# Score maximum in a spare PSUM column, sum scaling as a step, and an order of work drawn up anew: attention and a two-layer network on one core

## The chip, the cores and the metric

The kernel runs on one core of one Trainium2 chip. A core has five queues that run side by side, each in its own order: TensorE (PE in the profile, PEld for its weight loads), VectorE (DVE), ScalarE (ACT), GpSimd (POOL) and SyncE (SP), which here only issues transfers. Matmuls write their results into PSUM, all other tiles lie in SBUF. The metric is the device time of one execution in microseconds (us).

## The reference

Queries, keys and values have shape (4, 8, 768, 64): 4 batches, 8 heads, 768 positions, 64 numbers a head. Each query and key gets a bucket of 6 sign bits; a query attends only to keys of its own bucket. The attention output, reordered to 3072 rows of 512, goes through a network of 512 to 2048 to 512 with GELU between.

```python
q_bits = (np.einsum('bhsd,dk->bhsk', q, proj) > 0)      # k_bits alike
mask = q_bucket[:, :, :, None] == k_bucket[:, :, None, :]
scores = np.where(mask, scale * q @ k.T, -1000000000.0)
scores = scores - np.max(scores, axis=-1, keepdims=True)
attn = np.exp(scores)
attn = attn / (np.sum(attn, axis=-1, keepdims=True) + 1e-09)
x = (attn @ v).transpose(0, 2, 1, 3).reshape(B * S, H * D)
h = x @ w_in
g = 0.5 * h * (1.0 + erf(h / sqrt(2)))
return g @ w_out
```

## The kernel before, in words

**Score tiles.** One unit of attention (`unit`, L750) is 128 queries of one head against all 768 keys; there are 192 units. `scores` (L760) makes 2 x 2 matmuls into a score tile `s` in PSUM: two halves of 384 columns, each at the start of its own bank of 512, so that 128 columns of either bank are unused. There are two such tiles. The mask is part of the same matmuls: extra rows of the operands add 0 where the 6 bits agree and a large negative number, a multiple of `BIG / 2` = 2^33, where they don't. `top` (L767) is a DVE reduction over the tile, which writes the negated maximum `nm` into `rows`, a small SBUF tile of seven numbers a row. `guard` (L770) is a DVE instruction on two elements: it multiplies the pair (1, `nm`) by 1, or by 0 where `nm` shows that no key had the query's bucket, and so makes the scale `sc` and the bias `nb`. `exps` (L777) is the exponential on ACT, which takes both and also adds up the row's sum `ssum`; only then is the score tile free for another unit. `si` is the sum times a power of two plus the small constant, and `norm` (L785) its reciprocal `r` on DVE. The table `SI` (L30) says where `si` is computed: for batch 0 on ACT, in the same step as the exponential; for batches 1 to 3 on DVE, in the same step as the reciprocal.

**Two ways onward.** A unit of the "whole" kind (the four head pairs of the first pass and two of the second, `WHOLE`, L28) is transposed on PE against a diagonal that holds `r` (`whole_turn`, L825; matmuls of L834), copied out of PSUM (ACT or DVE), and multiplied with the values in fp32 (L882). Every other unit is split into a high and a low fp16 half (`high`, L790, on ACT, DVE or POOL; `low`, L793, on DVE), transposed by a transfer that SP issues (`turn`, L799, the DMA at L801), and multiplied with the values' halves (L891).

**Passes.** The first pass takes 256 queries of all 8 heads of batch 0, the second the other 512, three more take batches 1 to 3. Beside them the weights are loaded, decoded on DVE, scaled and split (`weight_pair`, L447; `w_in` in four jobs, then `w_out` in four, through three `wraw` buffers in that order), and the scale of the values is found (`v_scale`, L564). The network runs on groups of 256 rows and 8 blocks of the hidden layer: hidden matmuls (L1076), scaling out of PSUM on ACT (L1086), GELU (L1110, which needs another table on ACT than the exponential), a split of the result, output matmuls (L1144), and at the end of a row block `drain` (L1164) and `store`. The network of one batch fills PE while attention of later ones goes on; it needs all of `w_in` decoded for its first hidden matmul and all of `w_out` for its first output matmul.

**The order.** Nothing is scheduled by hand. Each step is given to a planner (`Plan`, L52) with a cost in us, what it needs, the buffer that it takes, and a key; a step that may run on several engines has a cost and a key offset for each. `order` (L91) plays the steps through with these costs: an engine that is free takes the ready step of lowest key. The instructions are then emitted in that order, so that each engine's queue is fixed in advance, and a queue whose next instruction isn't ready waits. The keys are a unit's running number (or a constant) plus offsets from `PAR` (L33). `HOP`, `SAME` and others are the plan's costs for handing on a result; `port` marks DVE steps that the plan keeps apart from POOL's.

Of the kernel before, what the change touches and what calls it, by code (L numbers as in the profile page):

```python
# [10 lines left out]
F32 = mybir.dt.float32  # L11
# [17 lines left out]
TABLE = 1.3  # L29
SI = ("ACT", "ACT", "DVE")  # L30
GROW = ("p","hl")

PAR = dict(Z=268.47, VS0=1.21, H0=215.64, HL=-15.55, VS=-265.71, G2=6.63, HQ=-12.55, VQ=-4.7, in0=-73.45, out0=510.52, in1=114.3, out1=-23.2, in2=-152.73, out2=90.41, in3=-266.67, out3=305.62, H1=156.76, H2=26.31, H3=-124.25, H4=-47.37, H5=96.79, H6=-21.71, H7=-18.75, MEV=-10, MGE=-10, MSP=-9, V0=28.21, QK0=31.02, QK1=11.42, QK2=-140.46, MX0=-80.33, MX1=9.9, MX2=-171.5, EX0=-27.01, EX1=10.79, EX2=61.01, NR0=17.61, NR1=-25.22, NR2=244.7, HI0=-71.29, HI1=35.16, HI2=6.43, LO0=-34.27, LO1=80.28, LO2=111.56, PV0=285.55, PV1=4.61, PV2=4.07, TR0=-68.6, TR1=51.33, TR2=-109.76, V1=-165.36, V2=-260.64, Sin0=88.02, Sin1=-15.33, Sin2=43.2, Sin3=-128.94, Sout0=71.1, Sout1=-10.94, Sout2=100.15, Sout3=-147.52, Lin=-134.59, Pin=-24.26, Qin=-42.42, Cin=-52.71, Min=-68.37, Lout=-123.13, Pout=189.72, Qout=-194.24, Cout=-82.99, Mout=284.13, G0=46.99, G1=276.82, G3=31.32, G4=-297.54, G5=-122.96, G6=-106.16, G7=-15.81, DUP0=-55.86, DUP1=-36.2, DUP2=101.92, LOW0=-29.55, LOW1=24.48, LOW2=24.75, PRJ0=106.61, PRJ1=8.12, PRJ2=140.3, MSK0=53.6, MSK1=-45.87, MSK2=-170.2, DI_ACT=152.6, DI_DVE=8.86, DI_Pool=-7.82, WS_ACT=62.38, WS_DVE=-70.95, WS_Pool=66.08, WH_ACT=24.68, WH_DVE=71.89, WH_Pool=-16.12, WL_ACT=167.53, WL_DVE=-13.6, WL_Pool=-46.06, VH_ACT=274.75, VH_DVE=33.02, VH_Pool=-33.68, MV_SP=-11.58, MV_ACT=170.85, MV_DVE=0.62, MV_Pool=-22.12, LO_ACT=16.2, LO_DVE=-202.51, LO_Pool=30.98, RND_ACT=-26.8, RND_DVE=128.78, RND_Pool=11.96, MSK_ACT=111.97, MSK_DVE=17.48, MSK_Pool=8.92, HI_ACT=-61.13, HI_DVE=-30.23, HI_Pool=15.87, DG_ACT=-0.18, DG_DVE=-102.45, DG_Pool=-90.6, EV_ACT=-12.47, EV_DVE=-6.28, EV_Pool=-230.2, GH_ACT=-45.74, GH_DVE=58.43, GH_Pool=56.03)  # L33
BIG = 2.0**34
# [3 lines left out]
class Step:  # L38
    def __init__(self, seq, engine, cost, emit, key, needs, takes, table, port):
# [5 lines left out]
        self.takes, self.table, self.port = takes, table, port  # L45
        self.needs = [n for n in needs if n is not None]
        self.slot = None
        self.frees = []
        self.start = self.end = None


class Plan:  # L52
# [14 lines left out]
    QUEUE = 2.0  # L67
    PORT = 0.1
    WINDOW = 3.413

    def __init__(self, rings):
        self.rings = {name: list(range(n)) for name, n in rings.items()}
        self.steps = []

    def add(self, engine, cost, emit, key, needs=(), takes=None, table=None, port=False):
        s = Step(len(self.steps), engine, cost, emit, key, needs, takes, table, port)
        self.steps.append(s)
        return s
# [12 lines left out]
    def order(self):  # L91
# [28 lines left out]
        port_at, port_of = 0.0, None  # L120
        warm, window, busy = False, 0, {}
        for t in set(free_at.values()):
            heapq.heappush(events, (t, -1, None))
        count = 0
        while events:
# [4 lines left out]
            for e in batch:  # L130
                if e is None:
                    continue
                for hold in e.frees:
                    hold["left"] -= 1
                    if not hold["left"]:
                        self.rings[hold["holder"].takes].append(hold["holder"].slot)
                for u in users.get(e, ()):
                    left[u] -= 1
                    for w in u.ways:
                        hop = self.SAME.get(w, 0.05) if w == e.engine else self.HOP[e.engine] + 0.12 * (w == "Pool")  # L140
                        at[u, w] = max(at.get((u, w), 0.0), now + hop)
                        heapq.heappush(events, (at[u, w], -1, None))
                    if not left[u]:
                        enlist(u)
            for engine, pool in ready.items():
# [3 lines left out]
                for s in pool:  # L149
                    if at.get((s, engine), 0.0) > now:  # L150
                        continue
                    if s.takes and not self.rings[s.takes]:
# [15 lines left out]
                if s.takes:  # L168
                    s.slot = self.rings[s.takes].pop(0)
# [24 lines left out]
                if engine == "SP":  # L194
                    free_at[engine] = now + 0.65
                    dma_at = max(dma_at, now + 1.0) + cost
# [19 lines left out]
def tile_bucket_attention_moe(  # L216
# [533 lines left out]
    def unit(t, i, q0, qs, cl, whole, made, place):  # L750

        aq, ak, bq, bk = sets[i]
        st = rows[:, t % NT]
        nm, sc, nb, ssum, si, r = (st[:, k : k + 1] for k in range(1, 7))

# [11 lines left out]
        def top():  # L767
            nc.vector.tensor_reduce(out=nm, in_=both(sp), axis=AX.XY, op=ALU.max, negate=True)  # L768

        def guard():  # L770

            nc.vector.scalar_tensor_tensor(  # L772
                out=st[:, 2:4], in0=nm.broadcast_to([P, 2]), scalar=BIG / 2, in1=st[:, :2],
                op0=ALU.is_lt, op1=ALU.mult,
            )

        def exps():  # L777
# [3 lines left out]
            )  # L781
            if si_on == "ACT":
                affine("ACT", si, ssum, unity, 1e-9 * unity)

        def norm():  # L785
            if si_on == "DVE":
                affine("DVE", si, ssum, unity, 1e-9 * unity)
            nc.vector.reciprocal(out=r, in_=si)
# [36 lines left out]
    def whole_turn(ex, nr, r, place, cl, t):  # L825
# [41 lines left out]
    def values(b, pr, ch, whole, vhl, turns, holds, key):  # L867
# [357 lines left out]
```

## Time and profile before

| What | Value |
|---|---|
| Three runs | 946.87, 948.25 and 949.5 us; median 948.25 |
| Profiled execution | span 946.1 us from the first to the last instruction; no other time is noted for it |
| PE busy | 874.5 us, 92% |
| DVE busy | 737.3 us, 78% |
| ACT busy | 595.7 us, 63% |
| POOL busy | 237.7 us, 25% |
| Last attention unit's exponential | starts at about 754 us |
| Mean granted clock of PE | 0.978 |

How to read the rows that follow in the prediction. A group's row names line, engine, operation, the tiles written and read, their shapes and the count; behind the first bar stand busy time in us and the mean of one in ns, behind the second the engine's idle time just before these instructions and what ended it. Many steps share the helper lines L382 (ACT) and L385 (DVE or POOL), so that the tile's name tells them apart. The row of a source line has the shortest, median and longest duration in ns, and the first and last start. A wait's row has who waited for whom, the total in us, how often, and the longest. A row of the timeline has start and duration in us.

### The profile page before, as it was taken

Reading aid. Unit: us, or ns where it says so; the run is one execution under the profiler, and the core shown is the slowest. Engines: PE = TensorE matmul, PEld = TensorE weight load, DVE = VectorE, ACT = ScalarE, POOL = GpSimd, SP = SyncE. Lnnn points to the kernel's source line nnn. Section 1 sums busy time; section 2 is a strip of 40 time slices with the busy share of each in tenths; the row PEclk is TensorE's granted clock in tenths of the full one; section 3 lists DMA queues with packets and bytes.
Section 4 is the critical chain, followed back from the end, with each engine's and each line's share of the span. In section 5 each row is a group of like instructions: output and inputs, shape, how many; then the busy total and the mean of one; then the engine's idle time right before and its main releaser. Section 6 shows DMA issues by size and latency. Waiting matters only on the chain. (4 is left out here: it accounts for less than half of the span.)

```text
span 946.1 us, 17526 instructions
## 1 busy us (share of the span) xinstructions
PE 874.5 (92%) x6656; PEld 636.7 (67%) x6656; DVE 737.3 (78%) x1455; ACT 595.7 (63%) x949; POOL 237.7 (25%) x230
## 2 busy tenths in 40 slices
PE   3764899969999999999999999999999999999998
PEld 2653787856767767687767676775777766676763
DVE  7989999998999999989899998899998822212122
ACT  5565677878777786778878766767776623222221
POOL 2321222344332433313324223222344200000000
PEclk9796999989999999999999999999999999999999
DMA  8575751588999799788988987869775830000000
GB/s 251 161 229 149 208 165 52 128 183 157 152 180 177 159 181 210 154 163 160 176 167 163 209 161 150 163 118 178 154 151 121 138 58 23 1 24 23 1 24 22
DMA packets 314628, 128.81 MB, mean 136 GB/s; under 512 B 254128, under 2 KB 298288, under 8 KB 314544
## 3 DMA queue, kind: packets, MB, share of 16 engines
q1 hardware_dynamic: 314368, 127.70, 64.0%
q8 instruction: 52, 0.85, 0.4%
q14 instruction: 32, 0.26, 0.1%
q10 hardware_dynamic: 176, 0.00, 0.0%
HBM read 45.49 MB, written 6.29 MB: 55 GB/s over the span
## 5 line engine op out<-in xcount | busy, mean ns | idle before, releaser
L1076 PE MATMUL hp<-x,Win 128*128 128x256 f16 x2304 | 268.6, 274 | 1.3 <-DVE x L918 0.7
L1144 PE MATMUL hp<-Wout,g 128*128 128x512 f16 x1152 | 262.3, 380 | 0.4 <-DVE g L1124 0.4
L1076 PEld LDWEIGHTS <-Win 128*128 128x128 f16 x2304 | 220.5, 98 | 43.8 <-issue 15.0
L1144 PEld LDWEIGHTS <-g 128*128 128x128 f16 x1152 | 108.4, 98 | 128.4 <-issue 9.3
L768 DVE TENSOR_REDUCE rows<-s 128x1 f32<-128x768 f32 x192 | 179.7, 949 | 7.9 <-PE s L765 6.8
L778 ACT ACTIVATE p<-s,rows 128x768 f32<-128x768 f32 x140 | 138.3, 988 | 43.3 <-DVE rows L772 28.5
L764 PE MATMUL s<-Ak,Aq 128*128 128x384 f32 x352 | 137.2, 390 | 17.5 <-ACT p L778 11.1
L1086 ACT ACTIVATE h<-hp,ffs 128x512 f32<-128x512 f32 x96 | 65.6, 683 | 118.8 <-PE hp L1076 118.3
L765 PE MATMUL s<-Bk,Bq 128*128 128x384 f32 x352 | 120.3, 342 | 0.0
L385 DVE TENSOR_SCALAR g<-h,ffs 128x512 f16<-128x512 f32 x33 | 18.5, 561 | 122.2 <-ACT h L1110 86.8
L764 PEld LDWEIGHTS s<-Ak,Aq 128*128 128x128 f32 x352 | 67.2, 191 | 42.7 <-ACT p L778 17.8
L891 PE MATMUL hp<-pt,vhl 128*64 128x256 f16 x1440 | 86.4, 274 | 4.5 <-DMA pt<-hl 2.3
L891 PEld LDWEIGHTS <-vhl 128*64 128x64 f16 x1440 | 76.5, 110 | 16.1 <-issue 12.5
L794 DVE SCALAR_TENSOR_TENSOR hl<-p,rows,hl 128x768 f16<-128x768 f32 x71 | 73.6, 1038 | 2.8 <-POOL hl L385 1.7
L1124 DVE SCALAR_TENSOR_TENSOR g<-h,ffs,g 128x512 f16<-128x512 f32 x96 | 72.3, 768 | 3.9 <-POOL g L385 1.1
L765 PEld LDWEIGHTS s<-Bk,Bq 128*128 128x128 f32 x352 | 67.7, 192 | 0.8
L385 POOL TENSOR_SCALAR hl<-p,rows 128x768 f16<-128x768 f32 x38 | 42.5, 1119 | 100.1 <-DMA pt<-hl 42.4
L834 PEld LDWEIGHTS hp<-dr,p 128*128 128x128 f32 x384 | 53.1, 218 | 20.2 <-ACT dr L382 9.9
L834 PE MATMUL hp<-dr,p 128*128 128x128 f32 x384 | 56.7, 308 | 10.5 <-POOL dr L385 6.3
L778 ACT ACTIVATE wraw<-s,rows 128x768 f32<-128x768 f32 x52 | 51.4, 988 | 18.6 <-DVE rows L772 9.2
L729 ACT ACTIVATE sign<-hp,off 44x256 f32<-44x256 f32 (+1 forms) x74 | 41.9, 574 | 29.6 <-PE hp L726 28.7
L772 DVE SCALAR_TENSOR_TENSOR rows<-rows 128x2 f32<-128x2 f32 x192 | 52.1, 277 | 1.0
(164 smaller groups left out, 1151.8 us busy)
## 6 DMA issues: line engine op xcount, KB each, us to landing
raw<-qk SPq DMA_DIRECT2D x29, 384.0 KB, 3.4
vraw<-v SPq DMA_DIRECT2D x26, 384.0 KB, 4.0
wraw<-w_in SPq DMA_DIRECT2D x16, 512.0 KB, 4.9
wraw<-w_out SPq DMA_DIRECT2D x16, 512.0 KB, 4.9
out<-o SPq DMA_DIRECT2D x12, 512.0 KB, 2.8
Bk<-Aq SPq DMA_DIRECT2D x18, 192.0 KB, 3.6
Ak<-Aq SPq DMA_DIRECT2D x18, 192.0 KB, 3.2
rawe<-qk SPq DMA_DIRECT2D x8, 384.0 KB, 4.7
```

Source lines behind the costliest of these rows:

```text
L385: on.tensor_scalar(out=out, in0=in_, scalar1=scale, scalar2=bias, op0=ALU.mult, op1=ALU.add)
L764: nc.tensor.matmul(to, aq[:, qs], ak[:, n], start=True, stop=False)
L765: nc.tensor.matmul(to, bq[:, qs.start - q0 : qs.stop - q0], bk[:, n], start=False, stop=True)
L768: nc.vector.tensor_reduce(out=nm, in_=both(sp), axis=AX.XY, op=ALU.max, negate=True)
L778: nc.scalar.activation(out=buf(ex).rearrange("p (b k) -> p b k", b=2), in_=both(sp), func=AF.Exp, scale=sc, bias=nb, accum_out=ssum,)
L794: nc.vector.scalar_tensor_tensor(out=buf(hi)[:, 1], in0=buf(ex), scalar=r, in1=buf(hi)[:, 0], op0=ALU.mult, op1=ALU.subtract,)
L834: nc.tensor.matmul(buf(step[0])[:, (k - k0) * P : (k - k0 + 1) * P], buf(ex)[:, words(k)], buf(dg), start=True, stop=True,)
L891: nc.tensor.matmul(pv[j * D : (j + 1) * D], buf(vh)[:, tv, kt, j * D : (j + 1) * D], buf(holds[j][0])[:, tp * KT + kt, :nt], start=kt == 0 ...
L1076: nc.tensor.matmul(buf(pair[0])[:, j * ch[1] : (j + 1) * ch[1]], win_hl[:, f0 // WB1, tw, pr, f0 % WB1 : f0 % WB1 + P], x[:, tx, pr, : ch[1]],
L1086: nc.scalar.activation(out=bufs["h"][0][:, 2 * fp : 2 * fp + 2, :nt], in_=buf(pair[0])[:, : 2 * nt].rearrange("p (j k) -> p j k", j=2), fu ...
L1124: nc.vector.scalar_tensor_tensor(out=gt[:, 1, s2, :nt], in0=h[:, s2, :nt], scalar=sg, in1=gt[:, 0, s2, :nt], op0=ALU.mult, op1=ALU.subtract,)
L1144: nc.tensor.matmul(buf(banks[u]).rearrange("p (c f) -> p c f", c=NWB), gt[:, tg, f, u * P : (u + 1) * P], wout_hl[:, :, tw, ft], start=ft ...
```

## The change

It has these parts:

- `top` writes the negated maximum into column 385 of the score tile itself, in PSUM; column 384 holds a 1.0, written into both tiles by DVE at the start. `guard` reads the pair from there as its second tensor; its first tensor is a constant SBUF pair `limit` of `BIG / 2`, and its scalar is the maximum's column. `rows` shrinks from seven numbers to five.
- Scaling the sum is a step of its own (`total`), between the exponential and the reciprocal, which the planner gives to ACT, DVE or POOL; `SI` goes.
- The plan's costs change: scores 0.72 to 0.7, fp32 transposes 0.214 to 0.223 a block, fp16 value matmuls 0.72 to 0.655, 0.09 for a switch of PE between those and all others, the transposing transfer 2.16 to 2.0 with 1.6 us of SP in place of 0.65 (all other transfers 0.55), another hop by engine (`HOPX`), and a buffer that comes free only one hop after its last reader.
- All offsets in `PAR` are others. With them every engine's order differs.

Which computations are done, and in what precision, stays the same.

```diff
-SI = ("ACT", "ACT", "DVE")
-PAR = dict(Z=268.47, VS0=1.21, H0=215.64, HL=-15.55, VS=-265.71, G2=6.63, ...
-    in0=-73.45, out0=510.52, in1=114.3, out1=-23.2, in2=-152.73, out2=90.41, in3=-266.67, out3=305.62, ...
-    QK0=31.02, ... MX0=-80.33, MX1=9.9, MX2=-171.5, ... Sin0=88.02, ...
+PAR = dict(SI0=289.56, SI1=-565.22, SI2=403.39, SI_ACT=-600, SI_DVE=-170.18, SI_Pool=36.23,
+    Z=135.98, VS0=600, H0=204.16, HL=-220.19, VS=-592.65, G2=360.64, ...
+    in0=370.71, out0=600, in1=535.3, out1=27.1, in2=-394.38, out2=235.52, in3=-469.93, out3=579.09, ...
+    QK0=548.05, ... MX0=-466.08, MX1=114.98, MX2=-557.52, ... Sin0=530.47, ...
+HOPX = {"PE": 0.0, "DVE": -0.0, "ACT": -0.05, "Pool": 0.23, "SP": 0.15}
...
-                        self.rings[hold["holder"].takes].append(hold["holder"].slot)
+                        at_ = now + self.HOP[e.engine]
+                        self.rings[hold["holder"].takes].append((hold["holder"].slot, at_))
...
-                        hop = self.SAME.get(w, 0.05) if w == e.engine else self.HOP[e.engine] + 0.12 * (w == "Pool")
+                        hop = self.SAME.get(w, 0.05) if w == e.engine else self.HOP[e.engine] + HOPX.get(e.engine, 0.0) + 0.12 * (w == "Pool")
...
                 if engine == "PE":
+                    cost += self.SWITCH * (s.half != half)
+                    half = s.half
...
-                    free_at[engine] = now + 0.65
+                    free_at[engine] = now + s.issue
...
-    rows = const.tile([P, NT, 7], F32, tag="rows", name="rows")
+    rows = const.tile([P, NT, 5], F32, tag="rows", name="rows")
...
-    nc.gpsimd.memset(rows[:, :, 0], 1.0)
+    limit = const.tile([P, 2], F32, tag="limit", name="limit")
+    nc.gpsimd.memset(limit, BIG / 2)
+    SPARE = S // 2
+    for t in bufs["s"]:
+        nc.vector.memset(t[:, SPARE : SPARE + 1], 1.0)
...
-        nm, sc, nb, ssum, si, r = (st[:, k : k + 1] for k in range(1, 7))
+        sc, nb, ssum, si, r = (st[:, k : k + 1] for k in range(5))
...
         def top():
-            nc.vector.tensor_reduce(out=nm, in_=both(sp), axis=AX.XY, op=ALU.max, negate=True)
+            nc.vector.tensor_reduce(out=buf(sp)[:, SPARE + 1 : SPARE + 2], in_=both(sp), axis=AX.XY, op=ALU.max, negate=True)
         def guard():
             nc.vector.scalar_tensor_tensor(
-                out=st[:, 2:4], in0=nm.broadcast_to([P, 2]), scalar=BIG / 2, in1=st[:, :2],
-                op0=ALU.is_lt, op1=ALU.mult,
+                out=st[:, :2], in0=limit, scalar=buf(sp)[:, SPARE + 1 : SPARE + 2],
+                in1=buf(sp)[:, SPARE : SPARE + 2], op0=ALU.is_gt, op1=ALU.mult,
             )
...
-            if si_on == "ACT":
-                affine("ACT", si, ssum, unity, 1e-9 * unity)
+        def total():
+            affine(su.engine, si, ssum, unity, 1e-9 * unity)
         def norm():
-            if si_on == "DVE":
-                affine("DVE", si, ssum, unity, 1e-9 * unity)
             nc.vector.reciprocal(out=r, in_=si)
...
-        sp = add("PE", 0.72, scores, t - PAR[f"QK{cl}"], made, takes="s")
+        sp = add("PE", 0.7, scores, t - PAR[f"QK{cl}"], made, takes="s")
...
-        ex = add("ACT", 0.98 + 0.23 * (si_on == "ACT"), exps, t - PAR[f"EX{cl}"], [sh], takes="p", table="exp")
+        ex = add("ACT", 0.98, exps, t - PAR[f"EX{cl}"], [sh], takes="p", table="exp")
-        nr = add("DVE", 0.07 + 0.2 * (si_on == "DVE"), norm, t - PAR[f"NR{cl}"], [ex])
+        su = add({e: (c, PAR[f"SI_{e}"]) for e, c in (("ACT", 0.23), ("DVE", 0.07), ("Pool", 0.16))}, 0, total, t - PAR[f"SI{cl}"], [ex])
+        nr = add("DVE", 0.07, norm, t - PAR[f"NR{cl}"], [su])
...
-        tr = add("SP", 2.16, turn, t + PAR[f"TR{cl}"], [lo, *hold[:1]], takes=None if hold else "pt")
+        tr = add("SP", 2.0, turn, t + PAR[f"TR{cl}"], [lo, *hold[:1]], takes=None if hold else "pt", issue=1.6)
...
-                add("PE", 0.214 * (k1 - k0), lambda ...: product(k0, k1, step), t + PAR[f"LO{cl}"], [dg], takes="hp")
+                add("PE", 0.223 * (k1 - k0), lambda ...: product(k0, k1, step), t + PAR[f"LO{cl}"], [dg], takes="hp")
...
-                    "PE", (0.9 if whole else 0.72) * nt / TC, ..., takes=None if n else "hp",
+                    "PE", (0.9 if whole else 0.655) * nt / TC, ..., takes=None if n else "hp", half=True,
```

More of the change, by code (lines that the diff above doesn't have):

```diff
@@ new lines @@
+PAR = dict(SI0=289.56, SI1=-565.22, SI2=403.39, SI_ACT=-600, SI_DVE=-170.18, SI_Pool=36.23, Z=135.98, VS0=600, H0=204.16, HL=-220.19, VS=-592.65, G2=360.64, HQ=36.42, VQ=-419.48, in0=370.71, out0=600, in1=535.3, out1=27.1, in2=-394.38, out2=235.52, in3=-469.93, out3=579.09, H1=527.91, H2=-321.61, H3=79.43, H4=449.56, H5=505.15, H6=277.36, H7=420.57, MEV=433.8, MGE=387.64, MSP=347.76, V0=582.83, QK0=548.05, QK1=-95.08, QK2=-470.18, MX0=-466.08, MX1=114.98, MX2=-557.52, EX0=-202.79, EX1=194.78, EX2=-11.92, NR0=223.22, NR1=-104.15, NR2=269, HI0=396.2, HI1=-476.56, HI2=409.28, LO0=507.4, LO1=291.25, LO2=395.17, PV0=548.55, PV1=499.49, PV2=45.4, TR0=-278.97, TR1=320.43, TR2=452.27, V1=-222.57, V2=-600, Sin0=530.47, Sin1=-600, Sin2=-206.79, Sin3=-204.7, Sout0=-293.17, Sout1=24.18, Sout2=426.41, Sout3=40.21, Lin=-306.18, Pin=233.47, Qin=-256.16, Cin=27.08, Min=-219.73, Lout=592.14, Pout=489.27, Qout=-465.81, Cout=27.6, Mout=146.07, G0=-62.95, G1=-73.22, G3=486.95, G4=-472.28, G5=54.41, G6=565.59, G7=-205.73, DUP0=45.38, DUP1=155.05, DUP2=-162.47, LOW0=432.39, LOW1=-135.42, LOW2=209.52, PRJ0=513.66, PRJ1=22.94, PRJ2=142.76, MSK0=185.96, MSK1=-399.14, MSK2=590.75, DI_ACT=305.84, DI_DVE=-107.45, DI_Pool=-220.1, WS_ACT=-600, WS_DVE=147.75, WS_Pool=446.41, WH_ACT=-418.38, WH_DVE=342.62, WH_Pool=-124.86, WL_ACT=29.63, WL_DVE=161.85, WL_Pool=-128.43, VH_ACT=-462.83, VH_DVE=81.56, VH_Pool=-9.85, MV_SP=518.36, MV_ACT=504.85, MV_DVE=-13.84, MV_Pool=511.1, LO_ACT=-600, LO_DVE=-2.05, LO_Pool=-600, RND_ACT=240.8, RND_DVE=35.59, RND_Pool=-145.02, MSK_ACT=453.53, MSK_DVE=279.08, MSK_Pool=586.93, HI_ACT=121.96, HI_DVE=351.82, HI_Pool=-341.52, DG_ACT=558.51, DG_DVE=46.22, DG_Pool=-132.65, EV_ACT=-260.46, EV_DVE=-26.08, EV_Pool=-59.11, GH_ACT=-21.44, GH_DVE=-600, GH_Pool=388.78)
@@ L38, with __init__ @@
 class Step:
-    def __init__(self, seq, engine, cost, emit, key, needs, takes, table, port):
+    def __init__(self, seq, engine, cost, emit, key, needs, takes, table, port, half=False, issue=0.55):
         many = isinstance(engine, dict)
@@ L45, in __init__ @@
         self.takes, self.table, self.port = takes, table, port
+        self.half, self.issue = half, issue
         self.needs = [n for n in needs if n is not None]
@@ L68, with add @@
     PORT = 0.1
+    SWITCH = 0.09
     WINDOW = 3.413
     def __init__(self, rings):
-        self.rings = {name: list(range(n)) for name, n in rings.items()}
+        self.rings = {name: [(k, 0.0) for k in range(n)] for name, n in rings.items()}
         self.steps = []
-    def add(self, engine, cost, emit, key, needs=(), takes=None, table=None, port=False):
-        s = Step(len(self.steps), engine, cost, emit, key, needs, takes, table, port)
+    def add(self, engine, cost, emit, key, needs=(), takes=None, table=None, port=False, half=False, issue=0.55):
+        s = Step(len(self.steps), engine, cost, emit, key, needs, takes, table, port, half, issue)
         self.steps.append(s)
@@ L121, in order @@
         warm, window, busy = False, 0, {}
+        half = False
         for t in set(free_at.values()):
@@ L135, in order @@
                     if not hold["left"]:
-                        self.rings[hold["holder"].takes].append(hold["holder"].slot)
+                        at_ = now + self.HOP[e.engine]
+                        self.rings[hold["holder"].takes].append((hold["holder"].slot, at_))
+                        heapq.heappush(events, (at_, -1, None))
                 for u in users.get(e, ()):
@@ L151, in order @@
                         continue
-                    if s.takes and not self.rings[s.takes]:
+                    if s.takes and not (self.rings[s.takes] and self.rings[s.takes][0][1] <= now):
                         continue
@@ L168, in order @@
                 if s.takes:
-                    s.slot = self.rings[s.takes].pop(0)
+                    s.slot = self.rings[s.takes].pop(0)[0]
                     head[s.takes] += 1
@@ L806, in unit @@
         unity = 1.0 if whole else 2.0**-15
-        si_on = SI[cl]
-        sp = add("PE", 0.72, scores, t - PAR[f"QK{cl}"], made, takes="s")
+        sp = add("PE", 0.7, scores, t - PAR[f"QK{cl}"], made, takes="s")
         mx = add("DVE", 0.87, top, t - PAR[f"MX{cl}"], [sp])
         sh = add("DVE", 0.07, guard, t - PAR[f"EX{cl}"], [mx])
-        ex = add("ACT", 0.98 + 0.23 * (si_on == "ACT"), exps, t - PAR[f"EX{cl}"], [sh], takes="p", table="exp")
+        ex = add("ACT", 0.98, exps, t - PAR[f"EX{cl}"], [sh], takes="p", table="exp")
         free(sp, [ex])
-        nr = add("DVE", 0.07 + 0.2 * (si_on == "DVE"), norm, t - PAR[f"NR{cl}"], [ex])
+        su = add({e: (c, PAR[f"SI_{e}"]) for e, c in (("ACT", 0.23), ("DVE", 0.07), ("Pool", 0.16))}, 0, total, t - PAR[f"SI{cl}"], [ex])
+        nr = add("DVE", 0.07, norm, t - PAR[f"NR{cl}"], [su])
         if whole:
@@ L850, in whole_turn @@
             step.append(
-                add("PE", 0.214 * (k1 - k0), lambda k0=k0, k1=k1, step=step: product(k0, k1, step), t + PAR[f"LO{cl}"], [dg], takes="hp")
+                add("PE", 0.223 * (k1 - k0), lambda k0=k0, k1=k1, step=step: product(k0, k1, step), t + PAR[f"LO{cl}"], [dg], takes="hp")
             )
@@ L902, in values @@
                 add(
-                    "PE", (0.9 if whole else 0.72) * nt / TC, lambda kts=kts: product(kts), key, [vh, vl, xt[b, ch], *turns, *parts],
-                    takes=None if n else "hp",
+                    "PE", (0.9 if whole else 0.655) * nt / TC, lambda kts=kts: product(kts), key, [vh, vl, xt[b, ch], *turns, *parts],
+                    takes=None if n else "hp", half=True,
                 )
```

1 line of the change is left out of this document (removed).

## The prediction

> **What bounds the kernel now.** I read the totals and the stages first. Outside the profiled span of 946.1 us lie 2.15 us, if the median of the three runs (948.25) stands for an execution like the profiled one; the sum below is made against 946.1 and those 2.15 are added at its end.
>
> ```profile
> span 946.1 us, 17526 instructions
> PE 874.5 (92%) x6656; PEld 636.7 (67%) x6656; DVE 737.3 (78%) x1455; ACT 595.7 (63%) x949; POOL 237.7 (25%) x230
> ```
>
> The stages, in columns of time, PE, PEld, DVE, ACT and POOL busy time with instruction counts, granted PE clock, DMA share and GB/s:
>
> ```profile
> 0.00:10.00 10.00, 0.95 (x3) 0.39 (x4) 4.66 (x11) 4.32 (x5) 3.75 (x14) 1.00 0.77 200
> 0.00:130.00 130.00, 87.10 (x587) 70.32 (x588) 113.37 (x236) 76.14 (x145) 33.24 (x48) 0.88 0.67 192
> 130.00:250.00 120.00, 107.52 (x845) 82.48 (x844) 113.54 (x226) 93.49 (x170) 41.53 (x42) 0.96 0.65 141
> 250.00:750.00 500.00, 488.85 (x3888) 357.70 (x3886) 459.48 (x913) 372.16 (x575) 160.50 (x139) 1.00 0.85 164
> 750.00:946.00 196.00, 191.05 (x1343) 126.18 (x1340) 50.92 (x83) 53.90 (x62) 2.44 (x2) 1.00 0.10 24
> ```
>
> TensorE sets the end. Its work is the same matmuls before and after the change, so only its idle time and its slow clock can be won. Idle, as length minus busy: 42.9 us in the first 130, 12.5 from 130 to 250, 11.2 from 250 to 750, 5.0 after that. The rest of the kernel matters as far as it feeds PE. In the first two stages DVE is the feeder and nearly full: behind its first 10 us (4.66 busy) it works 108.7 of 120 us, then 113.5 of 120. From 250 on the hidden and output matmuls fill PE whatever attention does. The waits of PE, first those to 100 us, then 100 to 250, then 250 to 760 (total, times, longest):
>
> ```profile
> PE s L764 <- ACT p L778: 7.6, 2, 6.8
> ...
> PE s L764 <- ACT wraw L778: 6.8, 2, 4.9
> ...
> PE s L764 <- ACT p L778: 3.1, 6, 1.0
> PE s L764 <- ACT wraw L778: 2.4, 3, 1.1
> ```
>
> The score matmul (L764) waits for the exponential that frees one of two score tiles, and that exponential waits for maximum and guard. How such a gap is made:
>
> ```profile
> 194.40 1.91 ACT L1110 ACTIVATE h<-h 128x2048 f32<-128x2048 f32 x1
> ...
> 195.08 2.59 POOL L405 TENSOR_TENSOR Bk<-raw,Aq 64x768 fp32r<-64x768 f32 x1
> ...
> 195.94 1.76 DVE L772 SCALAR_TENSOR_TENSOR rows<-rows 128x2 f32<-128x2 f32 x1
> 196.33 1.28 ACT L778 ACT_TABLE_LOAD   x1
> ...
> 197.63 0.99 ACT L778 ACTIVATE wraw<-s,rows 128x768 f32<-128x768 f32 x1
> ...
> 198.76 0.69 PE L764 MATMUL s<-x,x 128*128 128x384 f32 x1 [4.89 <-ACT wraw L778]
> ```
>
> A two-element guard took 1.76 us and ended when the POOL instruction did (197.67 and 197.70). Here GELU and a table load would have held ACT until 197.61 anyway.
>
> **The guard.**
>
> ```profile
> L772 DVE SCALAR_TENSOR_TENSOR rows<-rows x192: 135/156/1765, 15.4 to 751.9; 128x2 f32<-128x2 f32 x192
> L772 DVE SCALAR_TENSOR_TENSOR rows<-rows 128x2 f32<-128x2 f32 x192 | 52.1, 277 | 1.0
> L788 DVE RECIPROCAL rows<-rows x192: 140/164/167, 19.2 to 756.8; 128x1 f32<-128x1 f32 x192
> L1049 DVE TENSOR_SCALAR ffs<-inv,ffs x4: 209/239/598, 217.9 to 552.5; 128x4 f32<-128x4 f32 x4
> L1045 DVE TENSOR_SCALAR ffs<-ffs x4: 153/154/155, 84.2 to 552.2; 128x1 f32<-128x1 f32 x4
> L423 DVE TENSOR_REDUCE tiny<-hp 128x1 f32<-128x128 f32 x12 | 3.4, 285 | 0.7 <-PE hp L420 0.5
> L517 DVE TENSOR_REDUCE tiny<-hp 128x1 f32<-128x64 f32 x4 | 0.9, 217 | 0.0
> L594 DVE TENSOR_REDUCE tiny<-stat_v x4: 130/142/148, 19.3 to 543.0; 128x1 f32<-128x4 f32 x4
> ```
>
> Median 156, mean 277: 192 x 0.121 = 23.2 us of DVE time are waits beyond the median. The old guard has two tensor operands in SBUF; the reciprocal, with one, is never longer than 167. The new guard has one in SBUF (`limit`) and one in PSUM, so I expect it not to wait for POOL. Its new price: reduces out of PSUM give (285 - 217) / 64 = 1.06 ns an element, hence 153 for 4 elements, against 142 from SBUF: 11 for PSUM. A pointer instead of an immediate: 209 against 154, 55. Together 156 + 11 + 55 = 222, which I round to 220. Ends: 156 (no extra) and 321 (the mean of L1049's four, waits included; 192 x 0.321 = 61.6). DVE gains 192 x (277 - 220) = 10.9 us; ends 23.2 gained and 8.4 lost. The stall's next victim is the following two-operand instruction on DVE (L794, L1124), so I don't count more.
>
> On PE's path this is worth far less: between 250 and 760 the waits on the exponential are 3.1 + 2.4 = 5.5 us, and I take half, 3; of the 4.89 at 193.9 I take 2, since GELU covers most of it. Sum -5; ends 0 and -5.5 - 6.8 = -12.3. Elsewhere the filler matmuls hide it.
>
> **The maximum into PSUM.**
>
> ```profile
> L768 DVE TENSOR_REDUCE rows<-s 128x1 f32<-128x768 f32 x192 | 179.7, 949 | 7.9 <-PE s L765 6.8
> ```
>
> No row shows DVE writing PSUM. By the 11 ns above, either way, 192 x 0.011 = 2.1 us of DVE time; taken as 0 on the path, ends -2 and +2. The Trainium skill ("Perfetto Trace Analysis", Optimizing Scalar/DVE Operations) speaks against the change here: it puts DVE's access overhead at about 60 ns on SBUF and 125 on PSUM. By that rule maximum and guard would pay 65 each, as an estimate 25 us of DVE time, which eats the guard's gain; the reduces above show 11, so the trace doesn't bear it out for reads, and no row shows a write.
>
> **Sum scaling on its own.**
>
> ```profile
> L385 DVE TENSOR_SCALAR rows<-rows 128x1 f32<-128x1 f32 x144 | 21.4, 148 | 10.6 <-ACT p L778 7.1 <-ACT wraw L778 2.1
> L382 ACT ACTIVATE rows<-rows 128x1 f32<-128x1 f32 x48 | 9.8, 204 | 1.5
> L336 POOL MEMSET fold<- x1: 93/93/93, 1.4 to 1.4; 64x1 f32 x1
> L385 POOL TENSOR_SCALAR dr<-ident,rows x13: 375/470/1602, 19.6 to 168.7; 128x128 f32<-128x128 bf16 x13
> ```
>
> For batch 0 it was fixed to ACT behind the exponential, for the 144 later tiles to DVE ahead of the reciprocal, where DVE stood 10.6 us waiting for ACT. Now the planner picks ACT, DVE or POOL. With half of the 144 moved, DVE loses 10.7 us of work and some 5 of standing; on POOL one costs between 0.093 and 0.375, on ACT 0.204. A scaling queued behind GELU (1.91) and a table load (1.28) holds up its reciprocal, then the high half, low half, transpose and value matmuls, and the score tile not at all. Cover is the filler, from 250 on. PE's idle there is 11.2 of which 3 are spent: I take -1, ends -3 and +2 (4 such pile-ups of 3.2 us that reach PE for 0.5 each).
>
> **Start.** One POOL memset replaces another. Two one-column DVE memsets come ahead of L344, which waits for its load:
>
> ```profile
> L341 DVE MEMSET hash_hi<- x1: 122/122/122, 0.8 to 0.8; 128x76 f32 x1
> DVE praw L344 <- DMA praw<-proj: 1.1, 1, 1.1
> ```
>
> 2 x 0.122 lie in that 1.1: 0, or +0.24 without the cover.
>
> **The order.** All key offsets change, so every queue (SP's loads and transposes, POOL's shares) is dealt anew; the trace cannot show the result, only what is to be had. DVE also decodes the weights in the first 130 us, 9.9 us for one of the three decoding steps of `w_out` alone, and in such stretches PE starves (the first row is of the groups up to 130 us, the slices are as above, the last row is the first and last output weight load):
>
> ```profile
> L483 DVE SCALAR_TENSOR_TENSOR Wout<-wraw,Wout 128x512 int32<-128x512 int32 x14 | 9.9, 714 | 0.0
> ...
> 80.00:90.00 10.00, 4.41 (x16) 3.77 (x16) 9.90 (x19) 5.03 (x7) 2.63 (x2) 0.50 0.22 52
> 190.00:200.00 10.00, 3.94 (x45) 3.07 (x43) 9.73 (x16) 9.84 (x14) 5.42 (x5) 0.74 0.92 191
> 200.00:210.00 10.00, 7.36 (x71) 5.93 (x69) 9.14 (x16) 4.40 (x10) 4.12 (x5) 0.92 0.69 167
> 210.00:220.00 10.00, 9.83 (x58) 7.34 (x58) 8.64 (x21) 8.30 (x18) 2.94 (x3) 0.83 1.14 180
> 220.00:230.00 10.00, 8.97 (x86) 6.61 (x84) 9.18 (x20) 7.34 (x13) 5.21 (x4) 1.00 0.59 144
> ...
> L1144 PEld LDWEIGHTS <-g x1152: 95/98/102, 227.9 to 941.0; 128*128 128x128 f16 x192
> ```
>
> The new keys push weights back: `w_in`'s first pair from -73.45 to 370.71 (its second half 530.47 later), V's scale from 1.21 to 600, while first-pass heads and reciprocals stay early. That puts attention's fp32 matmuls sooner, as filler for PE while weights are prepared. What a denser order can win: after its first 10 us DVE stands 11.3 us up to 130; I take half, -5.5. The clock was granted at 0.88 and 0.96, which costs about 87.1 x 0.12 + 107.5 x 0.04 = 14.8 us; fewer gaps would return some, -2. The costs that were changed match the trace better (a transpose holds SP for a median of 1.71 us, the plan had 0.65 and now 1.6), which makes an order more likely to come out as planned:
>
> ```profile
> L801 SPq DMA_TRANSPOSE pt<-hl x108: 1274/1710/4244, 179.6 to 758.3; - x108
> ```
>
> Ends: -30, a little over half of the 55.4 us idle before 250; and +15, worked out in the rival below.
>
> **Sum.** 946.1 - 5 - 0 - 1 - 0 - 5.5 - 2 = 932.6, and 2.15 outside: 934.75, so 935, with 925 to 943 as this case's own range.
>
> **Rivals.**
> - *The start closes up further* (0.12): the order wins its whole 30 in place of 7.5: 935 - 22.5 = 912, at half of the excess about 920. For it speaks that 55.4 of 71.6 us idle lie before 250; against it, that DVE needs its weight work in any order.
> - *The guard comes out dear* (0.08): at 321 ns it gives back its 5 on the path: 940. Against it, rows of like size.
> - *Nothing moves* (0.10): PE was filled anyhow and the order's gains and losses cancel: 948. From 250 to 750 PE is idle in 2.2% only, which speaks for it. The same time comes if the guard still waits for POOL and the order is no better.
> - *Weights come too late* (0.25), slower: the second half of `w_in`'s first pair carries 370.71 + 530.47 = 901, behind even the last batch's maxima (557.52 + 191 = 749), so DVE prefers them whenever both are ready. Then the first output matmul, now at 228, slides. While PE had neither those nor fp32 attention, from 190 to 210, it was idle 6.06 + 2.64 = 8.7 of 20 us, but 0.2 and 1.0 in the two slices behind: 9.9 of 40, a quarter. A slide of 60 us costs 15: 948.25 - 6 + 15 = 957. The 6 are the guard's and the scaling's; the order pays off less from a slide of 24 us on (24 x 0.25 = 6), a first output matmul after 252. Against it: DVE takes what is ready, and attention's rings hold it back often.
>
> **How the numbers follow.** The forecast has 0.45, the others as given. The range runs from 918, inside the first rival, to 958, just past the slow one. A change of 0.3% is 2.8 us, about what a measurement of this kernel can tell. Faster by more: 0.45 + 0.12 + 0.08 = 0.65; within: 0.10; slower: 0.25.
>
> **What would show it.** Guard: its longest near its median, at 0.2 to 0.24; if it still ends with POOL instructions, that step is wrong. Maximum: a mean within 15 ns of 949. Scaling: rows on three engines, and the 10.6 us of standing gone. Order: PE idle before 250 below 48 us, the first output matmul no later than 228. The forecast is wrong if PE's idle before 250 grows, or if idle time appears between 250 and 750.

## The result, and the profile after

The changed kernel takes 923.83 us (median of 4 runs, 922.17 to 926.66) against 948.06 for the kernel before, measured beside it. The ratio is 0.9746, with a 95% interval of 0.9726 to 0.9766: 24 us faster, where the prediction had 13. It lies in the stated range (918 to 958), and 1.2 us below the likeliest case's own (925 to 943).

The totals of the page after:

```profile
span 921.4 us, 17533 instructions
PE 870.4 (94%) x6656; PEld 636.1 (69%) x6656; DVE 715.9 (78%) x1374; ACT 602.7 (65%) x982; POOL 267.3 (29%) x289
```

The stages after, columns as in the prediction (time, then PE, PEld, DVE, ACT and POOL busy, granted clock, DMA share, GB/s):

```profile
0.00:130.00 130.00, 97.27 (x685) 79.67 (x687) 116.20 (x261) 85.91 (x156) 42.41 (x61) 0.92 0.69 203
130.00:250.00 120.00, 111.56 (x872) 84.39 (x869) 112.54 (x226) 93.41 (x162) 50.05 (x50) 0.96 0.69 146
250.00:750.00 500.00, 494.65 (x3992) 362.94 (x3990) 446.96 (x824) 380.43 (x620) 174.82 (x178) 1.00 0.82 161
```

The span is 24.7 us shorter. PE's busy time fell by 4.1 (874.5 to 870.4), its idle time by 20.6 (71.6 to 51.0). Of the idle time, 10.2 went in the first 130 us (42.9 to 32.7), 4.0 from 130 to 250 (12.48 to 8.44), 5.8 from 250 to 750 (11.2 to 5.4), the rest behind. More than two thirds were thus won where the fp32 attention and the weights share DVE, as the prediction had it; DVE itself is as full there as before (116.2 us against 113.4 up to 130).

PE's waits after: first those to 100 us, then 100 to 250, then 250 to 760 (total, times, longest).

```profile
PE hp L731 <- DVE Aq L395: 7.4, 2, 7.1
PE s L774 <- ACT p L788: 4.3, 2, 3.4
PE s L774 <- DVE Ak L395: 4.2, 2, 3.4
...
PE s L774 <- ACT wraw L788: 3.8, 1, 3.8
PE s L774 <- ACT p L788: 3.4, 3, 1.8
...
PE s L774 <- ACT p L788: 3.8, 5, 1.5
PE s L774 <- ACT wraw L788: 0.6, 2, 0.4
```

From 100 us on the longest kind is still the same: scores for the exponential that frees a tile. To 100 us it fell from 7.6 to 4.3, from 250 on from 5.5 to 4.4, and between them it did not fall (6.8 before, 3.8 + 3.4 = 7.2 after). Together that is 4.0 of the 20.6. More went at the fp32 transposes that wait for their diagonal (`dr`): to 100 us they waited 10.3 before (6.3 for POOL, 4.0 for ACT) and 3.9 after (2.3 and 1.6). That part comes with the order: `order_alone`, below, has 3.6 already, `guard_alone` still 10.1.

The changed instructions, and those of DVE that read two SBUF tensors (groups and source rows after):

```profile
L782 DVE SCALAR_TENSOR_TENSOR rows<-limit,s x192: 195/214/224, 17.2 to 726.9; 128x2 f32<-128x2 f32 x192
L782 DVE SCALAR_TENSOR_TENSOR rows<-limit,s 128x2 f32<-128x2 f32 x192 | 40.2, 214 | 1.2
L778 DVE TENSOR_REDUCE s<-s 128x1 f32<-128x768 f32 x192 | 181.3, 957 | 11.3 <-PE s L775 10.6 <-ACT h L1095 0.3
L395 POOL TENSOR_SCALAR rows<-rows x62: 190/390/1459, 32.5 to 725.0; 128x1 f32<-128x1 f32 x62
L395 POOL TENSOR_SCALAR rows<-rows 128x1 f32<-128x1 f32 x62 | 27.7, 447 | 156.6 <-ACT p L788 127.7
L395 DVE TENSOR_SCALAR rows<-rows 128x1 f32<-128x1 f32 x61 | 9.1, 149 | 5.9 <-ACT p L788 4.1 <-ACT wraw L788 0.8
L392 ACT ACTIVATE rows<-rows 128x1 f32<-128x1 f32 x69 | 13.9, 202 | 1.8
L1133 DVE SCALAR_TENSOR_TENSOR g<-h,ffs,g 128x512 f16<-128x512 f32 x96 | 76.3, 813 | 2.9 <-POOL g L395 0.6
```

No guard is longer than 224 ns; before, one took 1765. The maximum costs 8 ns more into PSUM. The scalings are spread 69 on ACT, 61 on DVE and 62 on POOL, where one takes 447 ns on average.

### The profile page after: what moved, and what is told of

The parts are those of the page before. It is cut to its first block, busy times and chain, and to the rows that moved or that the text cites. A ratio compares the mean times of both kernels' runs of the same rounds, so it can differ in the third digit from the quotient of the medians.

```text
span 921.4 us, 17533 instructions
## 1 busy us (share of the span) xinstructions
PE 870.4 (94%) x6656; PEld 636.1 (69%) x6656; DVE 715.9 (78%) x1374; ACT 602.7 (65%) x982; POOL 267.3 (29%) x289
## 4 chain that ended last, share of the span: by engine, by line
PE 50%; DVE 5%; DMA 3%; ACT 2%; issue 1%; POOL 0%; ACTq 0%; DVEq 0%; POOLq 0%
PE hp L1153 20%; PE hp L1085 18%; PE hp L900 5%; PE s L774 3%; PE s L775 3%; DMA pt<-hl 2%; DVE s L778 1%; DVE hl L803 1%; ACT p L788 1%; DMA vraw<-v 1%; DVE wraw L803 1%; PE hp L731 1%; PE hp L733 0%; PE hp L736 0%; ACT wraw L788 0%
## 5 line engine op out<-in xcount | busy, mean ns | idle before, releaser
L778 DVE TENSOR_REDUCE s<-s 128x1 f32<-128x768 f32 x192 | 181.3, 957 | 11.3 <-PE s L775 10.6
L395 DVE TENSOR_SCALAR g<-h,ffs 128x512 f16<-128x512 f32 x39 | 21.8, 558 | 120.1 <-ACT h L1119 84.4
L900 PEld LDWEIGHTS <-vhl 128*64 128x64 f16 x1440 | 76.2, 110 | 11.1 <-issue 10.1
L803 DVE SCALAR_TENSOR_TENSOR hl<-p,rows,hl 128x768 f16<-128x768 f32 x75 | 77.5, 1038 | 7.2 <-POOL hl L395 4.2
L1133 DVE SCALAR_TENSOR_TENSOR g<-h,ffs,g 128x512 f16<-128x512 f32 x96 | 76.3, 813 | 2.9 <-POOL g L395 0.6
L395 POOL TENSOR_SCALAR rows<-rows 128x1 f32<-128x1 f32 x62 | 27.7, 447 | 156.6 <-ACT p L788 127.7
L395 POOL TENSOR_SCALAR hl<-p,rows 128x768 f16<-128x768 f32 x42 | 45.3, 1078 | 67.0 <-DMA pt<-hl 48.5
L415 POOL TENSOR_TENSOR Bk<-raw,Aq 64x768 fp32r<-64x768 f32 x23 | 43.9, 1908 | 32.1 <-ACT Aq L392 26.9
```

The source lines that it names most:

```text
L395: on.tensor_scalar(out=out, in0=in_, scalar1=scale, scalar2=bias, op0=ALU.mult, op1=ALU.add)
L778: nc.vector.tensor_reduce(out=buf(sp)[:, SPARE + 1 : SPARE + 2], in_=both(sp), axis=AX.XY, op=ALU.max, negate=True)
L803: nc.vector.scalar_tensor_tensor(out=buf(hi)[:, 1], in0=buf(ex), scalar=r, in1=buf(hi)[:, 0], op0=ALU.mult, op1=ALU.subtract,)
L900: nc.tensor.matmul(pv[j * D : (j + 1) * D], buf(vh)[:, tv, kt, j * D : (j + 1) * D], buf(holds[j][0])[:, tp * KT + kt, :nt], start=kt == 0 ...
L1133: nc.vector.scalar_tensor_tensor(out=gt[:, 1, s2, :nt], in0=h[:, s2, :nt], scalar=sg, in1=gt[:, 0, s2, :nt], op0=ALU.mult, op1=ALU.subtract,)
```

## The experiments

Ratios are to the kernel before, measured in turn on the same chip. "Idle" is PE's idle time in the profile (length minus PE busy) up to 130 us, from 130 to 250 and from 250 to 750; before it is 42.9, 12.5 and 11.2, after 32.7, 8.4 and 5.4.

| Run | Median us | Ratio (95%) | Idle |
|---|---|---|---|
| guard_alone | 942.80 | 0.9974 (0.9955 to 0.9992) | 41.2, 13.4, 9.0 |
| new_costs_old_offsets | 949.23 | 1.0027 (1.0008 to 1.0045) | 42.6, 7.6, 14.0 |
| new_offsets_old_costs | 948.82 | 1.0010 (0.9986 to 1.0034) | 41.5, 9.9, 15.7 |
| new_steps_old_offsets | 946.14 | 1.0004 (0.9975 to 1.0033) | 47.6, 8.9, 8.2 |
| order_alone | 935.55 | 0.9869 (0.9834 to 0.9905) | 34.4, 10.6, 10.0 |
| old_guard_new_order | 928.87 | 0.9818 (0.9794 to 0.9841) | 32.5, 8.0, 7.5 |
| scaling_fixed | 930.15 | 0.9833 (0.9809 to 0.9857) | 34.1, 10.8, 6.5 |
| batch0_scaling_on_act | 927.81 | 0.9800 (0.9768 to 0.9832) | 33.9, 10.6, 4.7 |
| later_scaling_on_dve | 924.46 | 0.9778 (0.9740 to 0.9815) | 33.0, 9.3, 4.6 |
| pool_scalings_to_dve | 923.43 | 0.9745 (0.9701 to 0.9789) | 32.7, 7.8, 3.2 |
| old_weight_offsets | 939.18 | 0.9936 (0.9909 to 0.9963) | 39.3, 8.6, 9.5 |
| offsets_shifted_by_3 | 925.46 | 0.9778 (0.9739 to 0.9816) | 34.6, 7.4, 6.0 |

The last run tells how much two series of one program differ. Played with the shifted offsets, the plan gives the same order as without the shift, each of the 3673 steps on the same engine and at the same place; the run is the changed kernel once more, in another series of measurements (its profile has the same 17533 instructions). It has 0.9778 where the result had 0.9746, so a difference of 0.3% between two runs of the table tells nothing.

Two theories stood against each other at first. A: the order brings most of the gain. B: the lighter instructions do.

### The guard alone, at the old order

The kernel before, with the change's hunks on `rows`, `limit`, the two memsets, `top` and `guard`, and nothing else; the plan has the same costs, so every engine's order is that of before.

> Only the maximum and the guard are changed as in the changed kernel; order, costs and scaling of the sum stay those of before. Theory A (the order brings most of the 24 us): PE is fed anyway, so that the 23 us of guard waits give 2 to 6 us, time 942 to 946, and other two-operand DVE instructions wait longer by some 10 us in all, as they do in the changed kernel. Theory B (the instructions bring most of it): 12 us or more, time 936 or less, at the same order.

It took 2.5 us off (0.8 to 4.3): theory A. PE's waits for the exponential hardly moved: 7.9 to 100 us, 6.9 from 100 to 250 and 4.8 from 250 on, where they had been 7.6, 6.8 and 5.5. The DVE groups of this run:

```profile
L776 DVE SCALAR_TENSOR_TENSOR rows<-limit,s 128x2 f32<-128x2 f32 x192 | 39.4, 213 | 1.1
L1128 DVE SCALAR_TENSOR_TENSOR g<-h,ffs,g 128x512 f16<-128x512 f32 x96 | 75.4, 800 | 4.4 <-POOL g L389 1.1 <-DVE g L389 0.5 <-ACT g L386 0.3
L798 DVE SCALAR_TENSOR_TENSOR hl<-p,rows,hl 128x768 f16<-128x768 f32 x71 | 75.3, 1061 | 1.4 <-POOL hl L389 1.2
L798 DVE SCALAR_TENSOR_TENSOR hl<-wraw,rows,hl 128x768 f16<-128x768 f32 x37 | 39.5, 1067 | 2.9 <-POOL hl L389 1.4 <-ACT hl L386 1.2
```

and the same groups before:

```profile
L1124 DVE SCALAR_TENSOR_TENSOR g<-h,ffs,g 128x512 f16<-128x512 f32 x96 | 72.3, 768 | 3.9 <-POOL g L385 1.1 <-ACT g L382 0.2
L794 DVE SCALAR_TENSOR_TENSOR hl<-p,rows,hl 128x768 f16<-128x768 f32 x71 | 73.6, 1038 | 2.8 <-POOL hl L385 1.7 <-ACT hl L382 0.9
L794 DVE SCALAR_TENSOR_TENSOR hl<-wraw,rows,hl 128x768 f16<-128x768 f32 x37 | 37.9, 1025 | 3.0 <-ACT hl L382 1.8 <-POOL hl L385 0.9
```

The guard's 52.1 us became 39.4. DVE's busy time fell by 5.7 only (737.3 to 731.6), so that 7.0 of those 12.7 came back: 3.1 at the split of GELU's result, 1.7 and 1.6 in two of the groups of low halves, and 1.2 at the maximum, which now writes PSUM. That fits a stall behind POOL that moves to other DVE instructions with two SBUF tensors, though the sum expected there was some 10. In the new order it goes elsewhere in part: between `order_alone` and `scaling_fixed`, which differ by the guard alone, the guard fell by 18.4 (58.4 to 40.0) and DVE's busy time by 7.5 (737.8 to 730.3), but the split of GELU's result did not grow (76.6 and 76.4).

### The new order with the old guard, and with the old place of the scaling

`old_guard_new_order` is the changed kernel with those hunks taken back: the order is that of after, instruction for instruction. `scaling_fixed` changes one line, so that each scaling stays at its place but on the engine of before; `order_alone` does both.

```diff
-            affine(su.engine, si, ssum, unity, 1e-9 * unity)
+            affine("DVE" if cl == 2 else "ACT", si, ssum, unity, 1e-9 * unity)
```

> The changed kernel's order, instruction for instruction, with the maximum in SBUF and the old guard. Theory A: 926 to 931, with guard waits back at about 20 us of DVE time. Theory B: 936 or more.

> The changed kernel at its own place for every scaling of the sum, but always on ACT in batch 0 and on DVE in the others, as before. Theory A: the free choice of engine is worth 0 to 3 us, time 924 to 927. Theory B: 930 or more, since DVE gets 144 scalings in place of 61. A third: POOL's 62 scalings, 447 ns each, block DVE's port; then it is faster than the changed kernel, 919 to 922.

> The changed kernel's order at every place, with all instructions of before: maximum and guard in SBUF, scaling on ACT for batch 0 and on DVE for the others. If the parts add up (guard 0.7%, scaling 0.9% of the new order), it keeps 1.0% of the gain: 10 us under the kernel before. If guard and scaling hide behind each other, 14 us or more under it. If the order lives by the new instructions: 5 us or less under it.

With the old guard in the new order the time is theory A's, though the guard's waits beyond the median come to 29 us (192 x (307 - 154) ns) where some 20 were expected. With the scaling's engines fixed it is theory B's by a hair (930.15). The order alone is 1.3% faster than before, some 12 us, about half of the gain; 10 were expected if the parts add up, 14 if they hide behind each other. Its stages:

```profile
0.00:130.00 130.00, 95.65 (x652) 78.10 (x653) 114.16 (x247) 84.24 (x165) 35.32 (x50) 0.91 0.69 201
130.00:250.00 120.00, 109.36 (x869) 83.08 (x868) 113.14 (x227) 93.68 (x174) 40.61 (x37) 0.97 0.66 140
250.00:750.00 500.00, 489.97 (x3890) 355.63 (x3889) 466.55 (x911) 373.73 (x572) 160.80 (x141) 1.00 0.81 161
```

On top of it the free scaling brings 0.5% (0.9869 to 0.9818) and the new guard another 0.7% (to 0.9746); in the other sequence the guard brings 0.4% (to 0.9833) and the scaling 0.9%. Together that is 0.9 to 1.2%, the smaller figure with the changed kernel's second series, and clear of the intervals. Each step by itself is about as large as the intervals, so which counts more isn't told. The guard's larger worth in the new order is less certain than it looks: the two profiled executions differ by 1.8 us (923.2 and 921.4), the medians by more. A fixed engine may also lose because the plan had dealt the order for another one; no run gives the scaling a fixed engine and an order of its own.

The verdict on A and B lies between them: order and instructions share the gain about evenly, but the instructions are worth little in the orders that the old offsets give.

### Costs, offsets and steps, each without the others

`new_costs_old_offsets` has the instructions and offsets of before, and the new plan costs. `new_offsets_old_costs` is the changed kernel with the old ones:

```diff
-HOPX = {"PE": 0.0, "DVE": -0.0, "ACT": -0.05, "Pool": 0.23, "SP": 0.15}
+HOPX = {}
-    SWITCH = 0.09
+    SWITCH = 0.0
-                        at_ = now + self.HOP[e.engine]
+                        at_ = now
-                    free_at[engine] = now + s.issue
+                    free_at[engine] = now + 0.65
...
```

`new_steps_old_offsets` has all of the change but the offsets, which are those of before, with 0 for the scaling's.

> Instructions and key offsets of before; only the plan's costs are the new ones. If better costs are what makes the order good: 930 to 940. If the offsets are what was fitted, and to the plan they were found with: 948 to 965, slower than before.

> The changed kernel with its new key offsets, but the plan's costs of before. Theory: offsets fit only the costs they were sought with, so the order is lost: 945 to 965, no faster than before. Rival: the offsets alone are the better ones: within 5 us of the changed kernel, 919 to 929.

> All new instructions, the scaling as a step of its own with offset 0 on each engine, and the new costs; the other key offsets are those of before. Theory A (the order, by its offsets, brings most): 938 to 952. Theory B (instructions and costs bring most): 932 or less.

None of the three is faster than before, though the last has every lighter instruction: its PE idles 47.6 us up to 130. Better costs alone don't give a better order, and the new offsets are good in the plan with the new costs and not in that with the old. Gain and order hang on costs, steps and offsets together. (The scaling's offsets of 0 in the last run are one choice; no other was tried.)

### Which scalings count

`batch0_scaling_on_act` and `later_scaling_on_dve` each do one half of `scaling_fixed`; `pool_scalings_to_dve` moves only POOL's 62. `batch0_scaling_on_act` moves 31 scalings to ACT (21 of POOL's, 10 of DVE's), `later_scaling_on_dve` 93 to DVE (52 of ACT's, 41 of POOL's).

```diff
-            affine(su.engine, si, ssum, unity, 1e-9 * unity)
+            affine("ACT" if cl < 2 else su.engine, si, ssum, unity, 1e-9 * unity)      # batch0_scaling_on_act
+            affine("DVE" if cl == 2 else su.engine, si, ssum, unity, 1e-9 * unity)     # later_scaling_on_dve
+            affine("DVE" if su.engine == "Pool" else su.engine, si, ...)               # pool_scalings_to_dve
```

> The changed kernel, with the scalings of batch 0 (21 on POOL and 9 on DVE among 45 in the profile) all put on ACT at their places; later ones as they are. If the 8 us that fixed engines cost come from batch 0, where ACT then holds up the start of the kernel: a ratio to before of 0.980 or more. If they come from the later batches: 0.977 or less.

> The other half: batch 0 free, the scalings of batches 1 to 3 (54 on ACT and 41 on POOL in the profile) all on DVE. If taking work off DVE is what counts: a ratio of 0.980 or more. If batch 0 is the cause: 0.977 or less. As POOL's share on DVE cost nothing, a loss here is the 54 that ACT does.

> The changed kernel with the 62 scalings that POOL does put on DVE, at the same places; the 69 on ACT stay. If POOL's 447 ns hold DVE's port and cost time: 919 to 922. If they are a relief for DVE, as the run with fixed engines lets one think: 927 to 930. Within 2 us of the changed kernel if only the ones on ACT mattered.

With batch 0's scalings all on ACT the ratio is 0.9800, just what was expected if batch 0 is the cause. With the later ones on DVE it is 0.9778, which neither expectation had, and which is the same as the changed kernel's own second series on that chip (`offsets_shifted_by_3`). So the times let batch 0 cost 0.2 to 0.5% and the later batches nothing that can be told; why the two together (`scaling_fixed`) lose 0.6 to 0.9% is open.

The traces say more. In the three runs with batch 0's scalings on ACT the score matmuls wait 14.4 to 14.5 us for exponentials up to 250 us, in the five with a free choice in batch 0 10.9 to 12.1. DVE stands before reciprocals for ACT's scaling; up to 210 us, first after, then with batch 0 on ACT:

```profile
DVE rows L797 <- ACT rows L392: 0.7, 2, 0.4
...
DVE rows L797 <- ACT rows L392: 4.6, 8, 1.3
```

So a late scaling holds up DVE, and with it, it seems, later maxima and the score tile; the chain from one to the other was not followed step by step.

POOL's 62 cost nothing that can be told on DVE: 0.9745, and PE then idles least of all from 250 on:

```profile
250.00:750.00 500.00, 496.85 (x4008) 364.24 (x4009) 451.12 (x858) 378.75 (x616) 160.11 (x140) 1.00 0.81 160
```

So POOL is neither relief nor harm here that can be told. As a kernel that run can't be told from the changed one.

### The weights' offsets, and a small shift of all

`old_weight_offsets` is the changed kernel with the 26 offsets of the weights (`in0` to `in3`, `out0` to `out3`, their `S`, `L`, `P`, `Q`, `C`, `M`) and `VS0` as before. `offsets_shifted_by_3` adds one line:

```diff
+PAR = {k: v + (3 if n % 2 else -3) for n, (k, v) in enumerate(PAR.items())}
```

> The changed kernel with the offsets of weight loading, decoding, scaling and of V's first scale as before; all others new. If moving the weights back is what makes the order better, as the prediction had it: a ratio of 0.99 or more, with PE idle time back before 250 us. If the weights' place matters little: 0.970 to 0.980.

> The changed kernel with every offset moved by 3 (three tiles' worth, against a range of 1200), up and down in turn. If the new offsets lie in a broad region of good orders: a ratio of 0.970 to 0.982. If they are one picked order among many worse ones: 0.985 to 1.01.

With the old weights' offsets two thirds to three quarters of the gain are gone (0.9936, against 0.9778 or 0.9746), and PE's idle time up to 130 us is back at 39.3. But more than the weights moves: the whole order is dealt anew, and 474 of the 3673 steps go to another engine. No run puts back another set of as many offsets, so that the loss may come from the weights' place or from any such disturbance. Moving every offset by 3 changes nothing in the order; whether orders near this one are as good is not shown.

What goes with the weights' place is seen in the rows of the `w_in` tile; before:

```profile
L1076 PE MATMUL hp<-x,Win x2304: 269/273/437, 133.7 to 923.2; 128*128 128x256 f16 x192
L473 DVE TENSOR_SCALAR Win<-wraw x12: 406/419/430, 19.9 to 61.5; 128x512 int32<-128x512 int32 x12
L544 DVE SCALAR_TENSOR_TENSOR Win<-Win,tiny x6: 1268/1276/1284, 39.2 to 82.0; 128x1024 f16<-128x1024 f32 x6
```

after:

```profile
L1085 PE MATMUL hp<-x,Win x2304: 269/273/421, 121.8 to 898.5; 128*128 128x256 f16 x192
L483 DVE TENSOR_SCALAR Win<-wraw x12: 407/417/520, 20.1 to 60.5; 128x512 int32<-128x512 int32 x12
L554 DVE SCALAR_TENSOR_TENSOR Win<-Win,tiny x6: 1271/1272/1276, 60.8 to 91.6; 128x1024 f16<-128x1024 f32 x6
```

and with the old weights' offsets in the changed kernel:

```profile
L1085 PE MATMUL hp<-x,Win x2304: 270/273/437, 134.6 to 914.7; 128*128 128x256 f16 x192
L554 DVE SCALAR_TENSOR_TENSOR Win<-Win,tiny x6: 1261/1272/1284, 39.7 to 77.4; 128x1024 f16<-128x1024 f32 x6
```

Decoding sits where it was. What moved back is the split of `w_in` into halves, by 10 to 22 us. And the first hidden matmul comes 12 us *earlier*: it needs not only `w_in`, ready by 100 us in all three, but the first pass's attention, and that finishes sooner when DVE does it ahead of the split. By 100 us DVE has done 16 maxima after, 12 before, 14 with the old weights' offsets; by 150 us 31, 26 and 27.

The other runs agree. `order_alone`, with every old instruction, has 16 and 30 maxima, the split from 62 us on and the first hidden matmul at 124.5. `new_offsets_old_costs` has the new weights' offsets, yet its split starts at 41 and its first hidden matmul comes at 134: far-back keys alone don't push the split back, the whole plan does. Late split, early first pass and a large gain go together in every run; none moves the split alone, so that it is the cause is argued.

## Why the prediction was right, point by point

**Guard.** It held in kind and size: 214 ns where 220 was forecast, no wait for POOL, 11.9 us of DVE time (52.1 to 40.2) where 10.9 was forecast. The price is right in part by luck: the 55 for a pointer set the shortest of one row (209) against the median of another (154), and by medians (239 and 153) it would have been 86. Its median grew by 58; no run takes pointer and PSUM apart. Its term on the path was 5. Alone it measured 2.5 in the old order; on the new one 0.4 to 0.7%, 3 to 7 us. The waits from which the 5 was taken gave little of it: with the guard alone the 5.5 from 250 on became 4.8, and the 4.89 behind GELU stayed 4.8. That 5 lies within 3 to 7 is thus luck in part too. The sentence that no more need be counted for the stall's next victim was mis-sized: in the run with the guard alone 7.0 of 12.7 us of DVE time came back, in the new order 8.4 of 17.9 and 10.9 of 18.4.

**Maximum into PSUM.** 957 against 949, 8 ns where 11 was forecast, and not the 65 that the prediction took as the difference of the two overheads in the Trainium skill ("Perfetto Trace Analysis", Optimizing Scalar/DVE Operations). The run does show a write now, and the row decides. For reads a row of before is more direct than the extrapolation to 4 elements: reductions over 768 took 946 ns from SBUF (L577) and 949 from PSUM (L768). For the guard the 65 isn't refuted, since 58 more were measured.

**Sum scaling.** This is the term that was most mis-sized: -1 forecast, 0.5 to 0.9%, 5 to 8 us, measured, against engines fixed in an order that was dealt for free ones. The step that failed is that only the 144 later tiles were counted, as work taken off DVE from 250 us on, and that a late scaling was said to hold up the score tile not at all. With batch 0 tied to ACT, PE's idle time up to 250 us is 44.5 in place of 41.2, and the score matmuls' wait for exponentials makes 3.0 of it (14.5 in place of 11.5). The 10.6 us of standing are not gone, as the prediction asked: 5.9 are left before DVE's scalings and 6.3 before the reciprocals (6.2 before). POOL's price went past its upper bound too (447 ns against 375), without cost that can be told.

**Start.** PE's longest wait at the start is 7.1 us where it was 7.4; the two memsets cost nothing that can be seen.

**Order.** -7.5 was forecast, and about -12 (9 to 16) measured for the order alone. The mechanism, weights back and attention's fp32 matmuls forward, fits the rows of all runs, with two corrections: only the split moved, and the new keys move it only together with the new costs. That it is what won the time is not shown by itself. The clock's part comes out well by the prediction's own working: 97.3 x 0.08 + 111.6 x 0.04 = 12.2 us of loss after, 14.8 before, 2.6 where 2 was forecast. But the same working gives 11.9 for the order alone, whose PE busy time did not fall (875.3 against 874.5), while after it fell by 4.1; so it is not shown either. That costs closer to the trace make a better order likely is not shown: by themselves they gave 1.0027.

**Rivals.** The first, a start that closes up further, is nearest (920), but its way isn't: idle time before 250 fell by 14.2, not by 30, and 5.8 came from the stage behind. The slow rival fell at its premise: the first output matmul came at 215 in place of 228, since a place far back in DVE's list of preferences didn't make the weights late: DVE takes what is ready, decoded `w_in` by 64 us in both kernels, and began the last decoding step of `w_out` at 183 us where it had been 191. The dear guard fell by the 214 ns, and that nothing moves by the 24 us.

```profile
L1153 PEld LDWEIGHTS <-g x1152: 95/98/102, 215.0 to 916.3; 128*128 128x128 f16 x192
```

## What to carry to other kernels

Ask of the first matmul that may fill PE which of its inputs comes last; here it was attention's first pass and not the weights, and work that wasn't due lay behind it in the faster orders. A wait behind another engine that is taken from one instruction comes back in part at others: here about half of it did, in three pairs of runs. Where the order is planned, test costs, offsets and steps each alone before crediting one of them; here costs alone and offsets alone gave nothing, and the guard alone 2.5 of the 24 us. And see that a small shift of the keys changes the order at all before taking it for a test of how lucky the order is.

## What the runs showed of the hardware

In the changed kernel a POOL instruction on one element a partition took 190 ns at least, 447 on average and up to 1459, while on DVE the same took 149 and on ACT 202. A DVE reduction that wrote its single result to PSUM instead of SBUF took 8 ns longer. A two-element DVE instruction with one tensor in SBUF and one in PSUM never took over 224 ns in the changed kernel (225 in the other runs that have it), while with both in SBUF it took up to 1795, in the run of the new order alone:

```profile
L778 DVE SCALAR_TENSOR_TENSOR rows<-rows x192: 130/154/1795, 16.7 to 740.6; 128x2 f32<-128x2 f32 x192
```
